# Two token streams, 64-row tail matmuls side by side, a convolution over four blocks transposed by DMA

## The chip, the cores and the metric

One Trainium2 chip, one core. The metric is device time in microseconds (us) for one execution; medians of several runs. One profiled execution of each kernel gives the trace; its span is from first to last instruction.

## The reference

Eight sequences of 4096 tokens with 192 channels. A causal convolution of 7 taps runs over time, each of 8 heads (24 channels) with its own softmaxed taps. Then a feed-forward layer with the activation h cos(h).

```
w   = softmax(weight)                                  # [8 heads, 7 taps]
out = einsum('hk,bskhg->bshg', w, windows_of_7(x))     # zero padding in front
h   = out @ w_in                                       # [32768, 192] x [192, 2048]
y   = (h * cos(h)) @ w_out                             # [2048, 192]
```

## The kernel before

A tile is 512 tokens. TensorE convolves with a banded matrix per head (one matmul for the block of 128 rows, one for what reaches into the next), transposes the result, multiplies it up in two parts of 96 channels, and multiplies it down. ScalarE takes the cosine as a shifted sine, VectorE the product.

```
    def conv_tile():
        # ... for each of 4 blocks s of 128 tokens, for each of 8 heads h:
                    nc.tensor.matmul(out=ct_ps[:, s2, h * G : (h + 1) * G], lhsT=band[:, h, :],
                                     rhs=x_bf[:, s, h * G : (h + 1) * G], start=True, stop=False)
                    nc.tensor.matmul(out=ct_ps[:, s2, h * G : (h + 1) * G], lhsT=bandhi[:, h, :],
                                     rhs=nxt[:, h * G : (h + 1) * G], start=False, stop=True)
        # ... copies to SBUF, then 8 transposes on TensorE and two copies back
    for it in range(NT):                                   # 64 tiles
        for f in range(NF):                                # 16 blocks of 128 hidden columns
            h_ps = h_ps_pool.tile([128, T], FP32)
            for c in range(2):
                nc.tensor.matmul(out=h_ps, lhsT=w_in_sb[:, c, f * 128 : (f + 1) * 128],
                                 rhs=conv_sb[:, c, :], start=(c == 0), stop=(c == 1))
            nc.scalar.activation(out=cos_sb, in_=h_ps, func=AF.Sin, bias=halfpi, scale=1.0)
            nc.vector.tensor_tensor(out=g_sb[:, f, :], in0=h_ps, in1=cos_sb, op=ALU.mult)
        # ... next tile's convolution, then 4 x 16 down matmuls of 192 columns
```

Of the kernel before, what the change touches and what calls it, by code (L numbers as in the profile page):

```python
# [12 lines left out]
ALU = mybir.AluOpType  # L14


@with_exitstack
def kernel(
# [7 lines left out]
):  # L26
    nc = tc.nc
# [3 lines left out]
    G = D // H  # L31
    T = 512
    NT = (B * S) // T
    TPB = S // T
    HD = D // 2
    NF = Dff // 128
    PAD = K - 1

    xf = x.rearrange("b s d -> (b s) d")

    consts = ctx.enter_context(tc.tile_pool(name="consts", bufs=1))
    xtp = ctx.enter_context(tc.tile_pool(name="xtp", bufs=1, space=bass.MemoryType.PSUM))
    pp = xtp

    ident = consts.tile([128, 128], BF16)
    make_identity(nc, ident)

    w_sb = consts.tile([H, K], FP32)
    nc.sync.dma_start(out=w_sb, in_=weight)
    wmax = consts.tile([H, 1], FP32)  # L50
    nc.vector.tensor_reduce(out=wmax, in_=w_sb, axis=mybir.AxisListType.X, op=ALU.max)
    negmax = consts.tile([H, 1], FP32)
    nc.vector.tensor_scalar(out=negmax, in0=wmax, scalar1=-1.0, scalar2=None, op0=ALU.mult)
    wexp = consts.tile([H, K], FP32)
    wsum = consts.tile([H, 1], FP32)
    nc.scalar.activation(out=wexp, in_=w_sb, func=AF.Exp, bias=negmax, scale=1.0)
    nc.vector.tensor_reduce(out=wsum, in_=wexp, axis=mybir.AxisListType.X, op=ALU.add)
    winv = consts.tile([H, 1], FP32)
    nc.vector.reciprocal(winv, wsum)
    wsm = consts.tile([H, K], BF16)  # L60
    nc.vector.tensor_scalar(out=wsm, in0=wexp, scalar1=winv, scalar2=None, op0=ALU.mult)
    cidx = consts.tile([H, H * K], FP32)
    nc.gpsimd.iota(cidx, pattern=[[1, H * K]], base=0, channel_multiplier=0, allow_small_or_imprecise_dtypes=True)
    hidx = consts.tile([H, 1], FP32)
    nc.gpsimd.iota(hidx, pattern=[[0, 1]], base=0, channel_multiplier=K, allow_small_or_imprecise_dtypes=True)
    tdiff = consts.tile([H, H * K], FP32)
    nc.vector.tensor_scalar(out=tdiff, in0=cidx, scalar1=hidx, scalar2=None, op0=ALU.subtract)
    ge0 = consts.tile([H, H * K], FP32)
    nc.vector.tensor_scalar(out=ge0, in0=tdiff, scalar1=-0.5, scalar2=None, op0=ALU.is_gt)
    ltK = consts.tile([H, H * K], FP32)  # L70
    nc.vector.tensor_scalar(out=ltK, in0=tdiff, scalar1=float(K) - 0.5, scalar2=None, op0=ALU.is_lt)
    hm = consts.tile([H, H * K], FP32)
    nc.vector.tensor_tensor(out=hm, in0=ge0, in1=ltK, op=ALU.mult)
    wsm_rep = consts.tile([H, H, K], FP32)
    for hh in range(H):
        nc.scalar.copy(wsm_rep[:, hh, :], wsm)
    wsm_exp = consts.tile([H, H * K], BF16)
    nc.vector.tensor_tensor(out=wsm_exp, in0=hm, in1=wsm_rep.rearrange("p a b -> p (a b)"), op=ALU.mult)
    ones8 = consts.tile([H, 128], BF16)
    nc.vector.memset(ones8, 1.0)  # L80
    wb_ps = xtp.tile([128, H * K], FP32)
    nc.tensor.matmul(out=wb_ps, lhsT=ones8, rhs=wsm_exp, start=True, stop=True)
    wb = consts.tile([128, H * K], FP32)
    nc.scalar.copy(wb, wb_ps)

    halfpi = consts.tile([128, 1], FP32)
    nc.vector.memset(halfpi, math.pi / 2.0)

    identx = consts.tile([128, 128 + K], BF16)
    nc.vector.memset(identx, 0.0)  # L90
    nc.gpsimd.tensor_copy(out=identx[:, 0:128], in_=ident)

    band = consts.tile([128, H, 128], BF16)
    bacc = consts.tile([128, 2, 128], FP32)
    btmp = consts.tile([128, 2, 128], FP32)
    eng = [nc.vector, nc.gpsimd]
    for h in range(H):
        b = bacc[:, h % 2, :]
        tmp = btmp[:, h % 2, :]
        nc.vector.tensor_scalar(out=b, in0=identx[:, 0:128], scalar1=wb[:, h * K : h * K + 1], scalar2=None, op0=ALU.mult)  # L100
        for k in range(1, K):
            e = eng[k % 2]
            e.tensor_scalar(out=tmp, in0=identx[:, k : k + 128], scalar1=wb[:, h * K + k : h * K + k + 1], scalar2=None, op0=ALU.mult)  # L103
            nc.vector.tensor_tensor(out=b, in0=b, in1=tmp, op=ALU.add)  # L104
        nc.scalar.copy(band[:, h, :], b)  # L105

    bandhi = consts.tile([128, H, 128], BF16)
    dmat = consts.tile([128, 128], FP32)
    nc.gpsimd.iota(dmat, pattern=[[1, 128]], base=0, channel_multiplier=-1, allow_small_or_imprecise_dtypes=True)
    mc = consts.tile([128, K - 1, 128], FP32)  # L110
    for ci in range(K - 1):
        nc.vector.tensor_scalar(out=mc[:, ci, :], in0=dmat, scalar1=float(122 + ci), scalar2=None, op0=ALU.is_equal)
    for h in range(H):
        b = bacc[:, h % 2, :]
        tmp = btmp[:, h % 2, :]
        nc.vector.tensor_scalar(out=b, in0=mc[:, 0, :], scalar1=wb[:, h * K + 6 : h * K + 7], scalar2=None, op0=ALU.mult)
        for ci in range(1, K - 1):
            e = eng[ci % 2]
            e.tensor_scalar(out=tmp, in0=mc[:, ci, :], scalar1=wb[:, h * K + 6 - ci : h * K + 7 - ci], scalar2=None, op0=ALU.mult)  # L119
            nc.vector.tensor_tensor(out=b, in0=b, in1=tmp, op=ALU.add)  # L120
        nc.scalar.copy(bandhi[:, h, :], b)  # L121

    w_in_f32 = consts.tile([HD, 2, Dff], FP32)
    for c in range(2):
        nc.sync.dma_start(out=w_in_f32[:, c, :], in_=moe_w_in[c * HD : (c + 1) * HD, :])
    w_in_sb = consts.tile([HD, 2, Dff], BF16)
    nc.scalar.copy(w_in_sb[:, 0, :], w_in_f32[:, 0, :])
    nc.scalar.copy(w_in_sb[:, 1, :], w_in_f32[:, 1, :])

    w_out_f32 = consts.tile([128, NF, D], FP32)  # L130
    nc.sync.dma_start(out=w_out_f32, in_=moe_w_out.rearrange("(n p) d -> p n d", p=128))
    w_out_sb = consts.tile([128, NF, D], BF16)
    nc.scalar.copy(w_out_sb, w_out_f32)


    xin = ctx.enter_context(tc.tile_pool(name="xin", bufs=3))
    xbf_pool = ctx.enter_context(tc.tile_pool(name="xbf", bufs=2))
    hx_pool = ctx.enter_context(tc.tile_pool(name="hx", bufs=2))
    ct_pool = ctx.enter_context(tc.tile_pool(name="ct", bufs=2))
    convT_pool = ctx.enter_context(tc.tile_pool(name="convT", bufs=2))  # L140
    cos_pool = ctx.enter_context(tc.tile_pool(name="cos", bufs=3))
    gpool = ctx.enter_context(tc.tile_pool(name="g", bufs=2))
    opool = ctx.enter_context(tc.tile_pool(name="o", bufs=3))
    ct_ps_pool = ctx.enter_context(tc.tile_pool(name="ct_ps", bufs=2, space=bass.MemoryType.PSUM))
    h_ps_pool = ctx.enter_context(tc.tile_pool(name="h_ps", bufs=3, space=bass.MemoryType.PSUM))
    o_ps_pool = ctx.enter_context(tc.tile_pool(name="o_ps", bufs=1, space=bass.MemoryType.PSUM))

    def prep_tile(it):
        t0 = it * T
        x_f32 = xin.tile([128, 4, D], FP32)  # L150
        if it % TPB == 0:
            nc.vector.memset(x_f32[0:PAD, 0, :], 0.0)
            nc.sync.dma_start(out=x_f32[PAD:128, 0, :], in_=xf[t0 : t0 + 128 - PAD, :])
            nc.sync.dma_start(out=x_f32[:, 1:4, :],
                              in_=xf[t0 + 128 - PAD : t0 + T - PAD, :].rearrange("(n p) d -> p n d", p=128))
        else:
            nc.sync.dma_start(out=x_f32, in_=xf[t0 - PAD : t0 + T - PAD, :].rearrange("(n p) d -> p n d", p=128))
        x_bf = xbf_pool.tile([128, 4, D], BF16)
        for s in range(4):
            nc.gpsimd.tensor_copy(out=x_bf[:, s, :], in_=x_f32[:, s, :])  # L160
        hx = hx_pool.tile([128, 2, D], FP32)
        nc.sync.dma_start(out=hx[0 : PAD, 0, :], in_=xf[t0 + T - PAD : t0 + T, :])
        nc.gpsimd.memset(hx[:, 1, :], 0.0)
        nc.gpsimd.tensor_copy(out=hx[0:PAD, 1, :], in_=hx[0:PAD, 0, :])  # L164
        hx_bf = hx_pool.tile([128, D], BF16)
        nc.gpsimd.tensor_copy(out=hx_bf, in_=hx[:, 1, :])  # L166
        state["x_bf"] = x_bf
        state["hx_bf"] = hx_bf

    def conv_tile():  # L170
        x_bf = state["x_bf"]
        convT = convT_pool.tile([HD, 2, T], BF16)
        ct_sb = ct_pool.tile([128, 4, D], BF16)
        for sp in range(2):
            ct_ps = ct_ps_pool.tile([128, 2, D], FP32)
# [24 lines left out]
    for it in range(NT):  # L200
# [12 lines left out]
        if it + 1 < NT:  # L213
            conv_cur = conv_tile()
            if it + 2 < NT:
                prep_tile(it + 2)
# [41 lines left out]
```

## Time and profile before

| | before |
|---|---|
| median of the timed runs | 1037.95 us |
| TensorE busy | 960.7 us, 93% of the span |
| VectorE, ScalarE busy | 80%, 70% |
| first up matmul starts | 72.5 us |
| up, down, convolution, transposes in the chain that ended last | 44, 34, 10, 4% |

A share of the chain times the span is the time that TensorE spends on that line with nothing else to wait for. The lines themselves are in the prediction.

### The profile page before, as it was taken

To read this page: it belongs to the slowest core of one execution; us is meant where nothing else is said; L and a number is where in the kernel's file an instruction comes from. 1 tells how busy PE (TensorE), PEld (TensorE's weight loads), DVE (VectorE), ACT (ScalarE), POOL (GpSimd) and SP (SyncE) were. 2 spreads that over 40 slices of the span, in tenths; PEclk is the share of its full clock that TensorE was granted. 3 is DMA by queue.
4 is the path that set the end of the run, shared out by engine and by line. 5 is a ranking of instruction groups with operands and counts; after the bars stand their busy time and mean duration, and the time that the engine had idled before them with its cause. 6 is when DMAs were issued, how large, how long until landed. Compare 5 with 4: busy or idle time off the path is not lost.

```text
span 1036.6 us, 26549 instructions
## 1 busy us (share of the span) xinstructions
PE 960.7 (93%) x10753; PEld 681.3 (66%) x10753; DVE 831.1 (80%) x1643; ACT 724.4 (70%) x1247; POOL 166.8 (16%) x506
## 2 busy tenths in 40 slices
PE   0039999999999999999999999999999999999997
PEld 0026677777777776777677677767776776777664
DVE  3658888888888888888788888888888888888885
ACT  3028777777777777777777777777677777777874
POOL 4651101110111111111101110111111011111100
PEclk9999999999999999999999999999999999999999
DMA  6001112211221122112111211121112112111010
GB/s 181 17 16 47 54 42 62 63 48 48 62 63 47 48 63 58 52 48 62 51 59 48 62 59 51 48 63 47 52 58 63 48 48 63 58 52 32 32 33 31
DMA packets 70748, 55.45 MB, mean 53 GB/s; under 512 B 2512, under 2 KB 70432, under 8 KB 70432
## 3 DMA queue, kind: packets, MB, share of 16 engines
q1 hardware_dynamic: 70624, 53.75, 17.2%
q8 instruction: 84, 1.38, 0.6%
q14 instruction: 40, 0.33, 0.1%
HBM read 28.57 MB, written 25.17 MB: 52 GB/s over the span
## 4 chain that ended last, share of the span: by engine, by line
PE 91%; POOL 3%; DVE 2%; ACT 1%; DMA 1%; issue 1%; SPq 0%; POOLq 0%
PE h_ps L207 44%; PE o_ps L224 34%; PE ct_ps L182 5%; PE ct_ps L180 5%; PE ps_t L191 4%; POOL btmp L119 1%; POOL btmp L103 1%; DMA w_in_f<-in_moe_w_in_dram 1%; DVE bacc L104 1%; ACT convT L192 0%; DVE bacc L120 0%; ACT cos_sb L210 0%; DVE btmp L103 0%; DVE g_sb L211 0%; DVE btmp L119 0%
## 5 line engine op out<-in xcount | busy, mean ns | idle before, releaser
L210 ACT ACTIVATE cos_sb<-h_ps,halfpi 128x512 bf16<-128x512 f32 x1024 | 660.4, 686 | 243.5 <-PE h_ps L207 222.1
L211 DVE TENSOR_TENSOR g_sb<-h_ps,cos_sb 128x512 bf16<-128x512 f32 x1024 | 667.8, 687 | 141.3 <-ACT cos_sb L210 131.2
L207 PE MATMUL h_ps<-convT,w_in_sb 96*128 96x512 bf16 x2048 | 579.1, 380 | 2.4 <-DVE g_sb L211 0.4
L224 PE MATMUL o_ps<-w_out_sb,g_sb 128*128 128x192 bf16 x4096 | 461.7, 246 | 2.6 <-DVE o_sb L226 1.3
L224 PEld LDWEIGHTS <-g_sb 128*128 128x128 bf16 x4096 | 352.1, 98 | 107.4 <-issue 18.1
L207 PEld LDWEIGHTS <-w_in_sb 96*128 96x128 bf16 x2048 | 185.6, 98 | 63.1 <-issue 5.4
L182 PEld LDWEIGHTS <-bandhi 128*128 128x128 bf16 x2048 | 126.0, 96 | 82.1 <-ACT bandhi L121 47.3
L160 POOL CAST x_bf<-x_f 128x192 bf16<-128x192 f32 x256 | 78.0, 343 | 597.2 <-PE ct_ps L182 597.2
L180 PEld LDWEIGHTS <-band 128*128 128x128 bf16 x2048 | 132.0, 96 | 54.8 <-ACT band L105 19.0
L180 PE MATMUL ct_ps<-x_bf,band 128*128 128x24 bf16 x2048 | 149.5, 174 | 16.2 <-ACT band L105 14.4
L182 PE MATMUL ct_ps<-x_bf,bandhi 128*128 128x24 bf16 x1536 | 116.8, 173 | 45.0 <-ACT bandhi L121 45.0
L226 DVE COPY o_sb<-o_ps 128x192 f32<-128x192 f32 x256 | 90.0, 352 | 24.3 <-PE o_ps L224 22.5
L191 PEld LDWEIGHTS <-ct_sb 128*96 128x96 bf16 x512 | 53.8, 123 | 42.4 <-ACT ct_sb L187 22.9
L191 PE MATMUL ps_t<-ident,ct_sb 128*96 128x128 bf16 x512 | 81.1, 231 | 0.1
L164 POOL COPY hx<-hx 6x192 f32<-6x192 f32 x64 | 21.4, 334 | 180.6 <-DMA hx<-in_x_dram 180.6
L185 DVE CAST ct_sb<-ct_ps 128x192 bf16<-128x192 f32 x128 | 43.5, 348 | 4.5 <-PE ct_ps L182 4.4
L187 ACT CAST ct_sb<-ct_ps 128x192 bf16<-128x192 f32 x128 | 40.5, 318 | 1.4 <-PE ct_ps L182 1.3
L192 ACT COPY convT<-ps_t 96x512 bf16<-96x512 bf16 x64 | 36.5, 570 | 1.0 <-PE ps_t L191 1.0
L182 PE MATMUL ct_ps<-hx_bf,bandhi 128*128 128x24 bf16 x512 | 36.0, 173 | 0.0
L193 DVE COPY convT<-ps_t 96x512 bf16<-96x512 bf16 x64 | 26.2, 410 | 0.0
L104 DVE TENSOR_TENSOR bacc<-bacc,btmp 128x128 f32<-128x128 f32 x48 | 13.4, 300 | 11.8 <-POOL btmp L103 11.6
L166 POOL CAST hx_bf<-hx 128x192 bf16<-128x192 f32 x64 | 22.0, 343 | 0.1
(45 smaller groups left out, 95.1 us busy)
## 6 DMA issues: line engine op xcount, KB each, us to landing
out_dram<-o_sb SPq DMA_DIRECT2D x64, 384.0 KB
x_f<-in_x_dram SPq DMA_DIRECT2D x56, 384.0 KB
x_f<-in_x_dram SPq DMA_DIRECT2D x8, 288.0 KB
w_in_f<-in_moe_w_in_dram SPq DMA_DIRECT2D x2, 768.0 KB
w_out_f<-in_moe_w_out_dram SPq DMA_DIRECT2D x1, 1536.0 KB
hx<-in_x_dram SPq DMA_DIRECT2D x64, 4.5 KB
x_f<-in_x_dram SPq DMA_DIRECT2D x8, 91.5 KB
w_sb<-in_weight_dram SPq DMA_DIRECT2D x1, 0.2 KB
```

Of the source, the lines that this page charges most:

```text
L160: nc.gpsimd.tensor_copy(out=x_bf[:, s, :], in_=x_f32[:, s, :])
L180: nc.tensor.matmul(out=ct_ps[:, s2, h * G : (h + 1) * G], lhsT=band[:, h, :], rhs=x_bf[:, s, h * G : (h + 1) * G], start=True, stop=False)
L182: nc.tensor.matmul(out=ct_ps[:, s2, h * G : (h + 1) * G], lhsT=bandhi[:, h, :], rhs=nxt[:, h * G : (h + 1) * G], start=False, stop=True)
L185: nc.vector.tensor_copy(out=ct_sb[:, s, :], in_=ct_ps[:, s2, :])
L187: nc.scalar.copy(ct_sb[:, s, :], ct_ps[:, s2, :])
L191: nc.tensor.transpose(ps_t[:, c, s, :], ct_sb[:, s, c * HD : (c + 1) * HD], ident)
L192: nc.scalar.copy(convT[:, 0, :], ps_t[:, 0, :, :])
L207: nc.tensor.matmul(out=h_ps, lhsT=w_in_sb[:, c, f * 128 : (f + 1) * 128], rhs=conv_sb[:, c, :], start=(c == 0), stop=(c == 1))
L210: nc.scalar.activation(out=cos_sb, in_=h_ps, func=AF.Sin, bias=halfpi, scale=1.0)
L211: nc.vector.tensor_tensor(out=g_sb[:, f, :], in0=h_ps, in1=cos_sb, op=ALU.mult)
L224: nc.tensor.matmul(out=o_ps[:, s2, 0:D], lhsT=g_sb[:, f, s * 128 : (s + 1) * 128], rhs=w_out_sb[:, f, :], start=(f == 0), stop=(f == NF - 1))
L226: nc.vector.tensor_copy(out=o_sb[:, s, :], in_=o_ps[:, s2, 0:D])
```

## The change

Its intent is to take work off TensorE. Two streams (sequence b and sequence b + 4) go through each step together. The 192 channels are split into 128 + 64. The two 64-row remainders, the "tails", lie on partitions 0 to 63 and 64 to 127 and use different row halves of the array at the same time. The convolution uses windows of 128 input rows for 112 outputs, so that one banded matrix does, over four windows in one matmul; the transposes become DMAs. Sine and product are 1024 wide. The order on every engine is set by hand.

```diff
+        xb = ... # [128 rows, 2 streams, 4 windows, 192]; windows step by 112 rows
+        nc.tensor.matmul(out=ps[:, :, h * G:(h + 1) * G], lhsT=band[:, h, :],
+                         rhs=xb[:, s, 0:nb, h * G:(h + 1) * G], start=True, stop=True)
+        nc.sync.dma_start_transpose(out=dst, in_=ct[0:rows, 0:cols])
-            nc.tensor.transpose(ps_t[:, c, s, :], ct_sb[:, s, c * HD : (c + 1) * HD], ident)
+    def up(n):
+        for s in range(2):
+            nc.tensor.matmul(out=h[:, s, :], lhsT=wA[:, f * 128:(f + 1) * 128], rhs=cT[b][:, s, t0:t0 + T],
+                             start=True, stop=False)
+        for s in range(2):
+            p = slice(s * DR, (s + 1) * DR)            # DR = 64
+            nc.tensor.matmul(out=h[:, s, :], lhsT=wR[p, f * 128:(f + 1) * 128], rhs=cT[b][p, 2, t0:t0 + T],
+                             start=False, stop=True)
+    for n in range(NSTEP + LAG):                       # 512 steps, down lags by 19
+        m = n - LAG
+        if n % 4 == 1: conv_part(...)
+        if n < NSTEP: up(n); sin(n)
+        if m >= 0: down(m)                             # 8 down matmuls
+        if 1 <= n <= NSTEP: mult(n - 1)
```

(Cut: loads, the band's building, the last 64 rows of a sequence, the output.)

## The prediction

> **What bounds the kernel now.** I read the page's busy shares first, then the slices, the chain that ended last, the costliest groups, and last the timeline of a few microseconds in the middle, because a matmul's busy time includes its latency and only start-to-start distances give its pace.
>
> ```profile
> span 1036.6 us, 26549 instructions
> PE 960.7 (93%) x10753; PEld 681.3 (66%) x10753; DVE 831.1 (80%) x1643; ACT 724.4 (70%) x1247; POOL 166.8 (16%) x506
> PE   0039999999999999999999999999999999999997
> PE 91%; POOL 3%; DVE 2%; ACT 1%; DMA 1%; issue 1%; SPq 0%; POOLq 0%
> PE h_ps L207 44%; PE o_ps L224 34%; PE ct_ps L182 5%; PE ct_ps L180 5%; PE ps_t L191 4%; POOL btmp L119 1%; POOL btmp L103 1%; DMA w_in_f<-in_moe_w_in_dram 1%; DVE bacc L104 1%; ACT convT L192 0%; DVE bacc L120 0%; ACT cos_sb L210 0%; DVE btmp L103 0%; DVE g_sb L211 0%; DVE btmp L119 0%
> ```
>
> TensorE is empty in the first slices (26 us each), then full to the end; the chain is TensorE's for 91%. By line: 44% up-projection, 34% down-projection, 10% convolution, 4% transposes: 456, 352, 104 and 41 us. The two elementwise engines wait for it, which the groups say:
>
> ```profile
> L210 ACT ACTIVATE cos_sb<-h_ps,halfpi 128x512 bf16<-128x512 f32 x1024 | 660.4, 686 | 243.5 <-PE h_ps L207 222.1
> L211 DVE TENSOR_TENSOR g_sb<-h_ps,cos_sb 128x512 bf16<-128x512 f32 x1024 | 667.8, 687 | 141.3 <-ACT cos_sb L210 131.2
> L226 DVE COPY o_sb<-o_ps 128x192 f32<-128x192 f32 x256 | 90.0, 352 | 24.3 <-PE o_ps L224 22.5
> L133 ACT CAST w_out_sb<-w_out_f 128x3072 bf16<-128x3072 f32 x1 | 2.8, 2752 | 2.7 <-DMA w_out_f<-in_moe_w_out_dram 2.7
> L127 ACT CAST w_in_sb<-w_in_f 96x2048 bf16<-96x2048 f32 x1 | 1.9, 1897 | 1.9 <-DMA w_in_f<-in_moe_w_in_dram 1.9
> ```
>
> The timeline gives the paces. The first stretch is one run of each kind on TensorE, the others are back-to-back runs on ScalarE and VectorE:
>
> ```profile
> 300.27 1.49 PE L224 MATMUL o_ps<-w_out_sb,g_sb 128*128 128x192 bf16 x16
> 301.59 1.46 PE L207 MATMUL h_ps<-convT,w_in_sb 96*128 96x512 bf16 x6
> 302.89 0.18 PE L180 MATMUL ct_ps<-x_bf,band 128*128 128x24 bf16 x1
> 302.92 0.17 PE L182 MATMUL ct_ps<-x_bf,bandhi 128*128 128x24 bf16 x1
> ...
> 407.13 1.84 ACT L210 ACTIVATE cos_sb<-h_ps,halfpi 128x512 bf16<-128x512 f32 x3 [1.19 <-PE h_ps L207]
> 408.85 0.33 ACT L187 CAST ct_sb<-ct_ps 128x192 bf16<-128x192 f32 x1
> ...
> 400.81 1.91 DVE L211 TENSOR_TENSOR g_sb<-h_ps,cos_sb 128x512 bf16<-128x512 f32 x3
> 402.63 0.35 DVE L226 COPY o_sb<-o_ps 128x192 f32<-128x192 f32 x1
> ```
>
> A down matmul (192 columns) costs (301.59-300.27)/16 = 82.5 ns, an up matmul (512) (302.89-301.59)/6 = 217 ns, a convolution matmul (24) about 25 ns, the mean over the next 28. No pause shows where 96-row weights follow 128-row ones. Three sines start (408.85-407.13)/3 = 573 ns apart though each lasts 686; three products (402.63-400.81)/3 = 607 ns. At these paces the down matmuls cost 4096 x 82.5 ns = 338 us and the up ones 2048 x 217 ns = 444, against the chain's 352 and 456: 3% more in use than alone.
>
> **What the Trainium skill says.** First, "TensorE: Matmul & The Clock Gate", Part 3 (row/col tiling): matmuls on different row groups run together, starting about 4 ns apart. The kernel before has no such pair, so its trace cannot agree or disagree. Second, "TensorEngine Tiling (Array Packing)", Key Properties: changing the tiling mode drains TensorE. If 64-row tiles count as another mode, each step pays two drains; not shown either, 96 to 128 rows being the nearest thing and free. Third, "ScalarE: Activation LUTs", What ACT_TABLE_LOAD costs: an ACTIVATE with a pointer bias takes 280 ns + 0.833 ns per element, and neighbours overlap by about 93 ns. The trace agrees: (2752-1897)/1024 = 0.835 ns per element between the two casts, 686 ns at 512 wide against 707, overlap 686-573 = 113 ns. Fourth, "VectorE: DVE Perf Modes", The three transpose paths: a 128x128 bf16 DMA transpose takes 1309 ns. No run yet shows it.
>
> **The change part by part.** A step is now 128 of the hidden columns for 2 x 512 tokens; there are 32 x 16 = 512 steps. The order of the built programs confirms, step by step, two 128-row and two 64-row up matmuls, then eight down matmuls, with a convolution part before every fourth step.
>
> *Up-projection.* 192 rows were 2 x 96, so 4 matmuls for 1024 tokens: 4 x 217 = 868 ns. Now 2 x 217 = 434 for the first 128 rows, and the 64-row tails of the two streams on different row halves and different PSUM banks: 217 + 4, I take 230. Together 664, a saving of 204 ns x 512 = 104 us. All on the path.
>
> *Down-projection.* The same 4096 matmuls: 8 x 82.5 = 660 ns a step. Nothing gained.
>
> *Convolution.* 4096 matmuls of 24 columns go (one for the band and one for what reaches over the block's edge), about 104 us, and the 512 transposes on TensorE with them, 41 us. In their place windows of 128 rows that give 112 outputs, four at once: per 448 tokens of both streams 10 matmuls of 96 columns, 2 of 32, 1 of 128 and 2 of 192. Between the measured 82.5 ns at 192 and 217 at 512 the slope is 0.42 ns per column, so 96 columns cost 42 ns, 128 cost 56, and 32 some 26 (24 columns took 25): 10 x 42 + 52 + 56 + 165 = 0.69 us, 36 times, with four short tails some 27 us, or 53 ns a step. Saving 104 + 41 - 27 = 118 us on the path. The copy after the transpose (36.5 us of ScalarE, 26.2 of VectorE) goes too; the transposes become 112 DMAs.
>
> *TensorE per step*: 664 + 660 + 53 = 1377 ns, and for switches between kinds some 2%, less than the 3% above as there are fewer: 1.405 us.
>
> *VectorE per step.* The slope from 192 to 512 wide is (687-352)/320 = 1.05 ns, so a 1024-wide product lasts about 687 + 536 = 1223 ns, and starts 607 + 536 = 1143 ns apart. Of 112 convolution parts 74 are copied out by VectorE, 512 wide, about 0.6 us each: 87 ns a step. Sum 1.23 us.
>
> *ScalarE per step.* 573 + 512 x 0.835 = 1.00 us apart; 38 convolution copies at 0.5 us are 37 ns a step; 128 output copies of 384 columns at about 0.38 us are 95 ns a step. Sum 1.13 us.
>
> So TensorE stays the bound, with VectorE 0.17 us a step behind. Three pairs of PSUM banks hold h. A new h waits for the product three steps earlier; up, sine and product in line take 0.66 + 1.11 + 1.22 us and about 0.4 for hand-overs, 3.4 us, against 4.2 for three steps. An output copy (0.48) and a convolution copy (0.68) in the same chain could use all of that slack, rarely.
>
> *Start.* Before, the first up matmul starts at 72.5 us, after two bands of 8 x 6 adds, alternated between VectorE and Pool. Now there is one band: 48 fused multiply-adds on VectorE, dependent one on the other, at 0.33 us each (a 128x128 add took 300 ns, plus a hand-over), and 8 products: 18 us. They wait for the exponential, which stands on ScalarE behind four weight casts, and so for 2.8 MB of loads; the 3 MB of weights before were cast by 18 us, so I take 15 us. Then masks and small work 3, band to 36, last convolution copies to 39, last transpose 3 us more: first up matmul at 42, 30 us earlier.
>
> *Sum.* 42 us; 19 steps without a down part, at VectorE's pace of 1.26 us: 24; 493 full steps x 1.405 = 693; 19 steps of down alone x 0.66 = 13; last copy and store 4.5, as before. That is a span of 777 us, and the timed runs lie 1.4 us above the span: about 778. I say 780.
>
> **The rivals.** *The 64-row pair does not run side by side, or drains.* Serial: +0.2 us a step, 512 x 0.2 = 102 us, so 880. Drains of about 0.06 us twice a step: +61 us, so 840. For it: the second page, and that nothing before tried it. Against: the first page, and that the hand-set order puts the pair's banks and row halves apart. *VectorE or the ring of h becomes the bound.* Then a step is 1.45 to 1.5 us, adding 493 x 0.07 = 35 us: about 815. For it: the product already has 80% here, and the slack is 0.17 us. Against: three buffers. *The transposes on the sync queue.* All loads, stores and transposes stand in one queue in order; 112 transposes have 6 us each. If issuing one takes over 6 us the queue is the bound, and 112 x 10 us would give 1100 or more. For it: no trace of one. Against: 1309 ns per 128x128 block from the page makes four blocks 5 us even one after the other, and DMA engines are 20% busy. *Gain hidden anyway*: ruled out, TensorE being full from 72 us on.
>
> **Range and chances.** The ideal pair (about 60%) gives 755 to 805, part drains or a VectorE bound (20%) 805 to 850, a serial pair (13%) 860 to 930, a queue bound (5%) over 1000. So 752 to 860 for 8 in 10. Faster by over 2% (under 1017): 0.95; within 2%: 0.02; slower: 0.03.
>
> **What would show it.** Right: first up matmul near 42 us; 16 steps every 22.5 us; starts of the two 64-row matmuls within some 20 ns; down matmuls still 82 ns apart; TensorE over 93% busy after 70 us, waiting little for the product. Wrong: 200 ns between the pair's starts, or gaps around it (first rival); TensorE waiting for the product of three steps earlier (second); TensorE or the copies waiting for DMA (third); VectorE's products over 1.25 us.

## The result, and the profile after

The changed kernel takes 870.27 us (869.39 to 871.25, four runs), against 1038.00 us of the kernel before in the same rounds: ratio 0.8384, 95% interval 0.8372 to 0.8396. All ratios and intervals here are from runs of the same rounds. The gain is 168 us where 258 were foretold, and 870 lies outside the range of 752 to 860.

The page of the changed kernel, in the same order as before:

```profile
span 869.1 us, 16182 instructions
PE 811.0 (93%) x6744; PEld 474.2 (55%) x6744; DVE 694.6 (80%) x656; ACT 642.4 (74%) x685; POOL 59.5 (7%) x51
...
PE   0158999999999999999999999999999999999998
...
PE 91%; DVE 5%; DMA 2%; ACT 1%; issue 1%; SPq 0%; ACTq 0%
PE misc L262 45%; PE h L234 25%; PE h L238 18%; DVE band L144 3%; PE misc L161 2%; DVE g L249 2%; DMA st<-in_moe_w_in_dram 1%; PE misc L171 1%; DMA cT<-ct 0%; DVE ct L223 0%; ACT cos L244 0%; PE misc L168 0%; DVE band L142 0%; PE misc L204 0%; PE misc L163 0%
...
L249 DVE TENSOR_TENSOR g<-h,cos 128x1024 bf16<-128x1024 f32 x512 | 625.1, 1223 | 128.5 <-ACT cos L244 122.8
L244 ACT ACTIVATE cos<-h,halfpi 128x1024 bf16<-128x1024 f32 x512 | 569.6, 1113 | 172.4 <-PE h L238 167.3
...
L238 PEld LDWEIGHTS <-wR 64*128 64x128 bf16 x1024 | 49.1, 93 | 217.7 <-issue 217.7
```

TensorE is still the bound: 91% of the chain, full from the fourth slice on. Sine and product last 1113 and 1223 ns, as foretold, and the sine waits for TensorE, the product for the sine, as before. The last line is new: 218 us in which the weight loader stood idle before the tail weights with nothing to wait for that the profile shows ("issue"), 512 times. That is not the loss itself, as matmuls stream during most of it; the timeline shows what is lost. The columns are start, duration of the merged group, engine, line, operation:

```profile
301.59 0.59 PE L234 MATMUL h<-cT,wA 128*128 128x512 bf16 x2
302.12 0.39 PE L238 MATMUL h<-cT,wR 64*128 64x512 bf16 x2
302.44 0.83 PE L262 MATMUL misc<-wo,g 128*128 128x192 bf16 x8
303.11 0.38 PE L161 MATMUL misc<-xb,band 128*128 128x96 bf16 x5
```

The two tails together last 0.39 us, and one of them alone lasts 0.39: they do run side by side (the single records have them 3 ns apart). But the first of them starts 0.53 us after the full-row pair, which streams for only 2 x 216 ns, and the down matmuls start 0.32 us after the tails, which stream for 216. The weight loader in the same microsecond:

```profile
302.12 0.10 PEld L238 LDWEIGHTS <-wR 64*128 64x128 bf16 x2 [0.42 <-issue]
302.44 0.11 PEld L262 LDWEIGHTS <-g 128*128 128x128 bf16 x2 [0.23 <-issue]
```

The weights of the first tail, and of the first down matmul behind it, are not loaded ahead: those of a full-row matmul or of the next down matmul start loading as soon as the matmul before them has started, but these start loading 0.31 to 0.32 us after it, and their matmul with them. The medians of start-to-start distances, from the single records of 493 steps: full row to full row 216 ns, full row to tail 312, tail to tail 3, tail to down 319, down to down 83. So going into 64-row tiles costs 312 - 216 = 96 ns and coming out 319 - 216 = 103 ns, 199 ns a step, when the pair saves 213.

The sum of the prediction, term by term:

| term | foretold | measured |
|---|---|---|
| first up matmul | 42 us | 53.8 us |
| 19 steps without down | 24 us | 25.3 us |
| 493 full steps | 693 us (1.405 us each) | 773.3 us (1.569 us each) |
| rest to the end | 17.5 us | 16.7 us |
| span | 777 us | 869.1 us |

And inside a full step, in ns:

| term | foretold | measured |
|---|---|---|
| two full-row matmuls | 434 | 432 |
| into the tails | with the next | 96 |
| the pair of tails | 230 | 219 |
| out of the tails | with the pair | 103 |
| eight down matmuls | 660 | 670 |
| convolution, mean | 53 | 49 |
| switches between kinds | 28 | 0 |
| sum | 1405 | 1569 |

The gain of 168 us (spans 1036.6 and 869.1) came from: the start, 72.5 - 53.8 = 19 us; convolution and transposes, from 10 + 4% of the chain, 145 us, to 512 x 49 ns = 25 us, so 120; the up-projection, from 456 us to 512 x 850 ns = 435, so 21; the down-projection, from 352 to 343, so 9.

### The profile page after: what moved, and what is told of

It reads as the page before. It is cut to its first block, busy times and chain, and to the rows that moved or that the text cites. A ratio compares the mean times of both kernels' runs of the same rounds, so it can differ in the third digit from the quotient of the medians.

```text
span 869.1 us, 16182 instructions
## 1 busy us (share of the span) xinstructions
PE 811.0 (93%) x6744; PEld 474.2 (55%) x6744; DVE 694.6 (80%) x656; ACT 642.4 (74%) x685; POOL 59.5 (7%) x51
## 4 chain that ended last, share of the span: by engine, by line
PE 91%; DVE 5%; DMA 2%; ACT 1%; issue 1%; SPq 0%; ACTq 0%
PE misc L262 45%; PE h L234 25%; PE h L238 18%; DVE band L144 3%; PE misc L161 2%; DVE g L249 2%; DMA st<-in_moe_w_in_dram 1%; PE misc L171 1%; DMA cT<-ct 0%; DVE ct L223 0%; ACT cos L244 0%; PE misc L168 0%; DVE band L142 0%; PE misc L204 0%; PE misc L163 0%
## 5 line engine op out<-in xcount | busy, mean ns | idle before, releaser
L249 DVE TENSOR_TENSOR g<-h,cos 128x1024 bf16<-128x1024 f32 x512 | 625.1, 1223 | 128.5 <-ACT cos L244 122.8
L244 ACT ACTIVATE cos<-h,halfpi 128x1024 bf16<-128x1024 f32 x512 | 569.6, 1113 | 172.4 <-PE h L238 167.3
L262 PE MATMUL misc<-wo,g 128*128 128x192 bf16 x4096 | 423.5, 247 | 0.0
L262 PEld LDWEIGHTS <-g 128*128 128x128 bf16 x4096 | 312.7, 98 | 111.6 <-issue 111.6
L234 PE MATMUL h<-cT,wA 128*128 128x512 bf16 x1024 | 305.7, 380 | 10.8 <-DMA cT<-ct 5.9
L238 PE MATMUL h<-cT,wR 64*128 64x512 bf16 x1024 | 200.1, 388 | 0.0
L234 PEld LDWEIGHTS <-wA 128*128 128x128 bf16 x1024 | 88.3, 98 | 15.0 <-DMA cT<-ct 6.6
L100 POOL CAST xb<-xw 128x1536 bf16<-128x1536 f32 x32 | 46.9, 1465 | 483.4 <-DMA xw<-in_x_dram 453.9
L267 ACT COPY osb<-misc 128x384 f32<-128x384 f32 x128 | 60.2, 470 | 10.3 <-PE misc L262 10.3
L161 PEld LDWEIGHTS <-band 128*128 128x128 bf16 x360 | 22.6, 100 | 39.2 <-DVE band L144 37.5
L95 POOL CAST xb<-xw 128x1536 bf16<-128x1536 f32 x4 | 5.9, 1463 | 61.6 <-DMA xw<-in_x_dram 43.3
L163 PEld LDWEIGHTS <-band 128*128 128x128 bf16 x72 | 7.2, 101 | 2.4 <-DVE band L144 2.4
```

The source lines that it names most:

```text
L100: nc.gpsimd.tensor_copy(out=xb, in_=xw)
L161: nc.tensor.matmul(out=ps[:, :, h * G:(h + 1) * G], lhsT=band[:, h, :], rhs=xb[:, s, 0:nb, h * G:(h + 1) * G], start=True, stop=True)
L234: nc.tensor.matmul(out=h[:, s, :], lhsT=wA[:, f * 128:(f + 1) * 128], rhs=cT[b][:, s, t0:t0 + T], start=True, stop=False)
L238: nc.tensor.matmul(out=h[:, s, :], lhsT=wR[p, f * 128:(f + 1) * 128], rhs=cT[b][p, 2, t0:t0 + T], start=False, stop=True)
L244: nc.scalar.activation(out=cos, in_=hs[n], func=AF.Sin, bias=halfpi, scale=1.0)
L249: nc.vector.tensor_tensor(out=g, in0=hs.pop(n), in1=cs.pop(n), op=ALU.mult)
```

## The experiments

Nine runs. Theory T: a change between 128-row and 64-row tiles costs about 0.1 us each way and ate the gain of the pair. Its rivals are named in the expectations. The changed kernel's 870.27 us is the yardstick; it was timed in other rounds, against the same kernel before (1038.0 us there, 1038.0 to 1038.5 in all rounds below).

**e1_pad128: no 64-row tiles at all.** The tail weights are padded with zero rows.

```diff
-    wR = consts.tile([128, Dff], BF16)
+    wR = consts.tile([128, 2, Dff], BF16)             # zeroed; stream s fills rows 64s..64s+63 of [:, s]
-            nc.tensor.matmul(out=h[:, s, :], lhsT=wR[p, f * 128:(f + 1) * 128], rhs=cT[b][p, 2, t0:t0 + T],
+            nc.tensor.matmul(out=h[:, s, :], lhsT=wR[:, s, f * 128:(f + 1) * 128], rhs=cT[b][:, 2, t0:t0 + T],
```

> The 64-row tail weights are padded with zero rows to 128, so that no matmul of the loop uses a 64-row tile; right result. Theory T (a change between 128-row and 64-row tiles costs about 95 ns each way, and the 64-row pair itself runs side by side): the 312 ns before the tail and the 319 ns behind it become 216 ns each, but the pair becomes two matmuls of 216 ns, so a step of 1569 ns becomes about 432 + 432 + 660 + 49 = 1573 ns: 872 us, the same within 1%. Rival P (the gaps belong to the place in the order, for instance a wait for the banks or for the tail data, not to the tile size): the two gaps stay, a step is about 1770 ns and the time about 970 us.

Correct; 873.02 us, ratio 0.8407. The timeline of this run:

```profile
300.58 0.59 PE L236 MATMUL h<-cT,wA 128*128 128x512 bf16 x2
301.01 0.60 PE L239 MATMUL h<-cT,wR 128*128 128x512 bf16 x2
301.44 0.82 PE L263 MATMUL misc<-wo,g 128*128 128x192 bf16 x8
302.10 0.59 PE L236 MATMUL h<-cT,wA 128*128 128x512 bf16 x2
```

The starts are 0.43, 0.43 and 0.66 us apart: both gaps are gone, and the tails take turns. Rival P has fallen. The whole side-by-side arrangement is worth 3 us (0.3%) against plain padding with zeros.

**e2_onetail: one tail left out** (wrong result).

```diff
-                             start=True, stop=False)
-        for s in range(2):
+                             start=True, stop=(s == 0))
+        for s in range(1, 2):
             p = slice(s * DR, (s + 1) * DR)
```

> Only one of the two 64-row tails is computed (the other stream's tail is left out; wrong result on purpose). Theory T: the pair runs side by side, so leaving one out saves 3 ns a step: 870 us, the same within 1%. Rival S (the two tails run one after the other, the starts 3 ns apart being only how they are recorded, and the 416 ns in excess of the full-row matmuls are simply 2 x 208): a step is 208 ns shorter, 106 us less, about 764 us.

877.36 us (two runs). Half of the tail work gone, and nothing gained: the pair is side by side, and rival S, which asked for 764 us, has fallen. In the loop the distance from product to product is 1564 ns against 1567 in the changed kernel, the 3 ns foretold. The 7 us too many are in the first steps. There the matmuls run at half pace:

```profile
66.02 1.04 PE L234 MATMUL h<-cT,wA 128*128 128x512 bf16 x2
66.99 0.61 PE L238 MATMUL h<-cT,wR 64*128 64x512 bf16 x1
```

The pair of full-row matmuls lasts 1.04 us instead of 0.59, and its second starts 0.40 us after the first instead of 0.22. Such steps stand from 53 to 90 us in this run, but only from 54 to 58 us in the changed kernel. The page's row of the granted clock shows 9 all along, which misleads: the clock record in the packed trace (no view prints it) begins, at full clock, only at 90.0 us in this run, 58.1 in the changed kernel and 97.1 in e3 below, and in each of them the pace changes at just that time. The page counts the stretch without a record as full clock. Why full clock came so late here is not shown. A lack of work is not the reason: TensorE is busy for 97% of 58 to 70 us here, and e1 and e3 give it more to do in each step, one as much as the other, yet full clock came at 58.7 us in e1 and later still in e3. Of the runs here only e2 and e3 let a tail stream with the other row half empty; whether that is the cause is untested.

**e3_samehalf: both tails on the same row half** (wrong result).

```diff
-            p = slice(s * DR, (s + 1) * DR)
+            p = slice(0, DR)
```

> Both tails use the rows 0 to 63 (wrong result on purpose for the second stream). Theory T: they can no longer run side by side; the second starts 216 ns after the first, since no tile change lies between them: +111 us, about 980 us. Rival S: no change, 870 us. Rival L (weights for 64-row tiles are never loaded ahead, whatever stood before): the second starts 312 ns after the first: +158 us, about 1028 us.

991.46 us (two runs). The timeline:

```profile
301.94 0.59 PE L234 MATMUL h<-cT,wA 128*128 128x512 bf16 x2
302.47 0.60 PE L238 MATMUL h<-cT,wR 64*128 64x512 bf16 x2
303.01 0.26 PE L262 MATMUL misc<-wo,g 128*128 128x192 bf16 x1
```

Now the two tails last 0.60 us: the second starts 226 ns after the first, 10 more than between full-row matmuls, and neither is slower by itself. So the row halves are what lets them run together, and a 64-row tile behind a 64-row tile pays no gap: rival L, which asked for 312 ns, has fallen. The cost belongs to the change of tile size. The step is 1781 ns, 213 more than 1567, which over 512 steps is 109 us of the 121 measured; the rest is again a longer stretch at half pace, to 97 us.

**e4_pairs: two steps joined, half as many tile changes.** The order on TensorE is full rows of n, tails of n, tails of n+1, full rows of n+1, 16 down matmuls. The lag becomes 20 and the g buffers 39; the convolution part stands before every second pair.

```diff
-    for n in range(NSTEP + LAG):
+    for n in range(0, NSTEP + LAG, 2):
-            up(n)
-            sin(n)
+            up(n, False)         # full rows, then tails
+            up(n + 1, True)      # tails first (they start the sum), then full rows
+            sin(n)
+            sin(n + 1)
         if m >= 0:
             down(m)
+            down(m + 1)
```

> Two steps are joined: full rows of step n, tails of n, tails of n+1, full rows of n+1, then 16 down matmuls. Half as many tile changes; right result. Theory T: 2 x 98 ns less in two steps, 512 x 98 ns = 50 us less: 820 us, perhaps 5 more for waits on the three h buffers. Rival L: the tail of n+1 starts 312 ns behind that of n, so one gap of the two saved comes back: about 845 us. Rival S: 870 us. If the three h buffers bind, TensorE waits for the product, and it is 850 or more with visible waits.

Correct; 818.47 us, ratio 0.7884, interval 0.7872 to 0.7896, which lies clear of the changed kernel's.

```profile
302.67 0.60 PE L242 MATMUL h<-cT,wR 64*128 64x512 bf16 x4
303.21 0.61 PE L236 MATMUL h<-cT,wA 128*128 128x512 bf16 x2
303.65 0.58 PE L269 MATMUL misc<-wo,g 128*128 128x192 bf16 x5
```

Four tails in 0.60 us, two pairs 223 ns apart, then the one gap that is left on the way out (308 ns to the full rows), and none before the down matmuls (216 ns behind the last full row). The gap on the way in stays (312 ns). The distance from product to product falls from 1567 to 1462 ns. This is theory T's number: the tile changes cost what they were said to cost.

**e5_expfirst: only the order of ScalarE at the start.** The block with the weight loads and casts is moved behind the softmax.

```diff
+    (softmax of the taps, up to wn)
     for c in range(2):
         st = stage.tile([128, HF], FP32, name="st")
         nc.sync.dma_start(out=st, in_=moe_w_in[0:DA, c * HF:(c + 1) * HF])
         nc.scalar.copy(wA[:, c * HF:(c + 1) * HF], st)
     ...
-    (softmax of the taps, up to wn)
```

> Only the order on ScalarE before the loop is changed: the exponential stands before the four weight casts instead of behind them, so that it runs at about 5.5 us instead of 18.8. If the late exponential alone made the first up matmul late (53.8 us instead of the 42 predicted), it comes 13 us earlier, at about 41 us, and the time is about 857 us. If something else ends last before it (the loads, the casts, the transposes in the queue), it gains less, and the first up matmul stays above 46 us.

Correct; 858.90 us, ratio 0.8272. The exponential runs at 5.4 us, the first up matmul at 41.9 instead of 53.8. The time falls by 11.4 us against the changed kernel's: of the 13.4 us by which the exponential is earlier, 11.9 reach the first up matmul.

**e6_nopool: no casts on Pool while the band is built.** As e5, and the casts of two input units and of the down weights go to ScalarE. In the changed kernel the lines of VectorE and Pool, in order of time, were:

```profile
21.15 4.60 DVE L144 SCALAR_TENSOR_TENSOR band<-mask,wn,band 128x128 bf16<-128x128 bf16 x6
...
25.95 4.45 DVE L144 SCALAR_TENSOR_TENSOR band<-mask,wn,band 128x128 bf16<-128x128 bf16 x6
...
30.60 2.29 DVE L144 SCALAR_TENSOR_TENSOR band<-mask,wn,band 128x128 bf16<-128x128 bf16 x6
```

```profile
21.02 1.47 POOL L100 CAST xb<-xw 128x1536 bf16<-128x1536 f32 x1 [11.85 <-DMA xw<-in_x_dram]
23.37 1.47 POOL L151 CAST wo<-st 128x1536 bf16<-128x1536 f32 x1 [0.88 <-DMA st<-in_moe_w_out_dram]
25.77 1.47 POOL L151 CAST wo<-st 128x1536 bf16<-128x1536 f32 x1 [0.94 <-DMA st<-in_moe_w_out_dram]
27.98 1.51 POOL L100 CAST xb<-xw 128x1536 bf16<-128x1536 f32 x1 [0.73 <-DMA xw<-in_x_dram]
```

Two heads of six multiply-adds take twice as long as the third, exactly while Pool casts. In the single records four of those twelve last 1432 to 1533 ns, the others 350; the four take about as long as one whole cast. The Trainium skill, "SBUF — State Buffer", SBUF: two separate sides, describes a port pair that VectorE, with two SBUF inputs, and Pool lock against each other for a whole instruction; these numbers agree.

```diff
-    load_unit(0, 1)
+    load_unit(0, 1, on_act)                 # the same for unit 2
-        nc.gpsimd.tensor_copy(out=wo[:, ...], in_=st)
+        nc.scalar.copy(wo[:, ...], st)
```

> The run before, and the casts that Pool makes while VectorE builds the band (two input units and the down weights) move to ScalarE. In the profile of the changed kernel the first two heads of the band took 4.6 us for six multiply-adds while Pool was casting, the other six 2.29 us. If Pool's casts slow them, all eight heads take 2.3 to 2.5 us, and the first up matmul comes up to 4.6 us earlier than in the run before (36 to 38 us, about 853 us in time). If the cause lies in the first heads themselves, they stay at 4.6 us.

Correct; 854.90 us, ratio 0.8237, 4.0 us under e5. Seven of the eight heads take 2.29 us, and only the first, beside the one cast that stayed on Pool, 3.37. The band is ready 4.7 us earlier than in e5 (28.5 against 33.2 us), the first up matmul only 2.8 us (39.1), because the copies of the convolution on ScalarE now stand behind the casts.

**e7_start: the start in full.** As e6; the second input unit is loaded before the weights; the first six parts go in the order 0a, 0b, 1a, 1b, 0r, 1r (units 0 and 1, a and b the 128 channels of each stream, r the tails), five of their copies on ScalarE; the third unit and the down weights (these cast on Pool again) are loaded behind the first transposes.

```diff
+    parts[:6] = [(0, 0, 0), (0, 0, 1), (0, 1, 0), (0, 1, 1), (0, 0, 2), (0, 1, 2)]
-        if k % 3 == 0:
+        if k < 5 or (k > 5 and k % 3 == 0):
```

> The start in full: exponential first, no Pool casts beside the band, the four 128-channel convolution parts before the two of the last heads, their copies on ScalarE, the second input unit loaded before the weights, and the down weights loaded after the first transposes. Band ready at about 28 us, first up matmul at about 34 us, 20 us earlier than in the changed kernel: about 850 us, unless the later loads make the first steps wait (then 855 to 860).

Correct; 854.52 us, ratio 0.8231: no better than e6, though the first up matmul starts at 29.0 us. The gain turned into a new wait. The first sine starts at 39.6 us, because the cast of the late third unit stands before it on ScalarE and waits for its DMA:

```profile
36.82 1.47 ACT L107 CAST xb<-xw 128x1536 bf16<-128x1536 f32 x1 [7.83 <-DMA xw<-in_x_dram]
38.31 1.28 ACT L241 ACT_TABLE_LOAD   x1
39.60 1.11 ACT L241 ACTIVATE cos<-h,halfpi 128x1024 bf16<-128x1024 f32 x1
```

**e8_both: e7's start with e4's pairs.**

> The start of the run before and the paired steps of e4 together. The two savings lie in different stretches, so they should add: 818 - 20 = about 798 us.

Correct; 803.43 us, ratio 0.7741. e4 and e7 save 51.8 and 15.8 us against the changed kernel's 870.27, together 67.6; both at once save 66.8. They add. The forecast of 798 had put the start at 20 us, where e7 brought 15.8.

**e9_best: the third unit earlier.**

```diff
+    load_unit(0, 2, on_act)                 # behind the tail weights
     band = consts.tile([128, H, 128], BF16)
 ...
     for k in range(6):
         conv_part(misc[k % 2])
-    load_unit(0, 2, on_act)
```

> As e8, but the third input unit is loaded behind the tail weights and cast on ScalarE before the convolution copies. In e7 its cast stood in front of the first sine, which began at 39.6 us though the first up matmul began at 29.0. If that cast held the first sine back, the first sine starts near 34.5 us and the time is about 5 us under e8's, 798 us. If not, it stays at 803 us.

Correct; 797.33 us (796.96 to 797.66, five runs), ratio 0.7676, interval 0.7666 to 0.7687. The first sine starts at 33.5 us. This is the fastest version, 73 us under the changed kernel.

## Why the prediction was wrong

**The bound.** Right. TensorE stayed the bound, and the paces taken from the timeline before held: 216 ns for 512 columns, 83 for 192, and 49 ns a step for the convolution where 53 were foretold. The convolution's saving was foretold as 118 us and is 120.

**The step that failed.** "217 + 4, I take 230. Together 664, a saving of 204 ns x 512 = 104 us." The pair costs 219 ns, as said, but the two changes of tile size around it cost 199 ns more, so the up-projection takes 850 ns instead of 664, and 95 of the 104 us did not come. The sign of it named beforehand, gaps around the pair, is what the trace shows. I had the reason in hand as the first rival, took it for the less likely one, and sized it at 0.06 us twice; it is 0.10 us twice (e1 takes both away, e4 one of two, and both times the time follows). The prediction leaned on the kernel before, where 96-row and 128-row weights follow one another without a gap. That was no evidence: the 80-row matmuls of the changed kernel's last convolution parts show no gap either (83 ns behind the last down matmul), and only the 64-row ones do. The Trainium skill, "TensorEngine Tiling (Array Packing)", Key Properties, had said that a change of tiling mode drains TensorE, without a figure; the gaps here fit it.

**The start.** Foretold 42 us, measured 53.8. Three terms: the exponential at 18.8 us instead of 15, behind the casts (e5 puts it at 5.4 us, earlier than foretold too, and gains 11.4 us); 48 multiply-adds at 0.45 us, not 0.33, 0.39 us apart when left alone and held by Pool's casts otherwise (e6: 4.0 us); and 8.4 us from the last band to the first up matmul instead of 6, as the queue issues six transposes in turn, 1.2 us each, with two loads between.

**The other rivals.** The ring of three h buffers did not bind in the full steps. In the waits of TensorE in the changed kernel the product appears with 4.9 us in all, all of it between 59.8 and 79.0 us, when there is no down part:

```profile
PE h L234 <- DVE g L249: 4.9, 12, 0.8
```

The transposes did not bind either: 112 of them land in 2.4 us each (the 5 us in the prediction was an estimate, from the 1309 ns of the page that it cites), and TensorE waited for one once, 5.9 us, before the first up matmul:

```profile
cT<-ct SPq DMA_TRANSPOSE x112, 2.4
...
L224 SPq DMA_TRANSPOSE cT<-ct x112: 1177/1197/1992, 41.3 to 714.7; - x112
```

The first line is from the issues on the page (median to landing in us), the second from the view of one source line (least, median and most ns that an issue holds the queue).

**The range.** A chance of 20% for "part drains or a VectorE bound" with a top of 850 was too small, and too low at the top: the drains I sized at 840 are 199 ns x 512 = 102 us in truth, and the late start adds 12. That the span came out only 92 us over the 777 is partly luck: the 28 ns a step kept for switches were not needed and the pair took 11 ns less, which over 493 steps gave 19 us back.

**What stays open.** Whether the 0.1 us is the array running empty or the weight load that cannot go ahead, or both in turn, these runs do not separate: load and matmul start together behind the gap. Why full clock came so late in e2 and e3 is open too.

## What to carry to other kernels

Packing two half-height matmuls side by side paid here only where several pairs stood together: each change of tile size cost half of what a packed pair of 512 columns saved, so two changes per pair left nothing, and padding with zeros was as good. Group the packed matmuls of several steps (tails first in one step, last in the next) to halve the changes. At the start, look for the small instruction that everything waits for and put it ahead of long casts in its engine's order, and keep Pool idle while VectorE runs a chain with two SBUF inputs.

## What the Trainium skill lacked or had wrong

- "TensorEngine Tiling (Array Packing)", Key Properties, says that changing the mode drains TensorE but gives no cost. Here it is 96 ns into and 103 ns out of 64-row tiles. Its row modes of 128, 64 and 32 fit the runs: 64 rows count as a change, 80 and 96 do not.
- "TensorE: Matmul & The Clock Gate", Part 3, gives packed matmuls starting about 4 ns apart (3 ns here, agreeing) and speedups for packed runs. It does not warn that between full-row matmuls the gain goes: 219 + 199 ns for the packed pair, against 432 for the padded one. It has weights loaded ahead where the row groups do not conflict or a background buffer takes them. Here full-row weights are loaded ahead behind full-row matmuls, but across a change of tile size none are (they start 307 ns after the last full-row matmul started).
- "VectorE: DVE Perf Modes", The three transpose paths, gives 1309 ns for one 128x128 DMA transpose. A 112x512 one landed in 2.4 us here; that its issue holds the queue for 1.2 us is on no page that I found.
- No page that I found warns that a trace's clock record can begin late, so that a clock row made from it shows full speed before: in e2 it begins at 90.0 us, and until then full-row matmuls of 512 columns start 381 to 426 ns apart, not 216.
